# Gated linear attention, mixture of experts and SwiGLU on one core: raw weight buffers in three pools, the token-number scatters moved, idle products in the attention's tail

## The chip, the cores and the metric

The kernel runs on one core of a Trainium2 chip. The metric is the time of one execution in microseconds (us) on the device. Its engines are TensorE (PE), VectorE (DVE), ScalarE (ACT), GpSimd (POOL) and SyncE (SP), which here does nothing but issue transfers; each runs its own list of instructions in the order in which the program wrote it, and they wait for one another by semaphores. Beside them sixteen DMA engines move data between DRAM and the on-chip memory.

## The reference

Three stages, each fed by the one before: a recurrence with a decay per channel, a layer of experts in which each token goes to one expert, and a SwiGLU.

```python
def _attn_ref(r, k, v, w, u):          # 2 batches, 8 heads, 768 steps, 48 channels
    for t in range(S):
        cur = np.einsum('bhd,bhe->bhde', u[None] * kt, vt)
        y[:, :, t] = np.einsum('bhd,bhde->bhe', rt, state + cur)
        state = wt[:, :, :, None] * state + np.einsum('bhd,bhe->bhde', kt, vt)

def _moe_ref(x, w_gate, w1, w2, capacity):   # 1536 tokens x 384, 8 experts, 1024 hidden
    expert_idx = np.argmax(logits, axis=1)
    # each token takes the next row of its expert, as long as there is room
    h = np.maximum(np.einsum('ecd,edf->ecf', disp, w1), 0.0)
    y = np.einsum('ecf,efd->ecd', h, w2)
    out[i] = gate_w[i] * y[expert_idx[i], pos[i]]

def _moe2_ref(x, w_gate, w_val, w_out):      # 384 -> 1536 -> 384
    g = x @ w_gate
    silu = g * (1.0 / (1.0 + np.exp(-g)))
    return (silu * (x @ w_val) @ w_out).astype(np.float32)
```

The SwiGLU's three weight matrices arrive as 8-byte floats, all else as 4-byte ones. The result is to be as exact as float32, so each large product is made from values split in two: a high part that the fast product form takes whole, and a low part, the rest. Three products (high by high, low by high, high by low) stand for one.

## The kernel before

**The attention** works through twelve chunks of 128 tokens, six of each batch, numbered u from 0 to 11. For a chunk it loads the decay data (tiles `dm`, in turn three buffers, L291 to L295) and the values (`v`, L301), forms running products of decays on DVE (`prep1`, L325, and `prep2`, L368 to L381, which ends with the tile `rk`) and checks them, makes scores (`scores`, L415, cut to the triangle by POOL in L418), reads the state (`values`, L438 and L442), brings it forward (`state`, L454), and adds the token's own term (`own`: POOL multiplies the values by a column per head into `aV`, L395; `xrow`, L479, adds `aV` to the chunk's product on DVE, which gives the row block x). `gate_t` (L495 to L507) transposes x on PE and copies it with ACT to `xT`; in the same tile of PE's memory it can make, from `rk` and from an earlier chunk's `xT`, rows of two other results: the logits of that chunk and the columns that `own` needs (L495). `diag` (L388) makes those columns alone, 2 wide. `columns` (L526) turns the rows round. `logits` (L521) makes a chunk's logits the plain way, 8 wide. `warm` (L404) issues products whose result nobody reads.

**The choice of expert.** Chunks are grouped: 0 to 3, 4 to 7, then the pairs 8 and 9 (`two`) and 10 and 11 (`last`). For a group, DVE takes the largest logit and the weights of the choice (`choose`, from L561), PE counts the tokens of each expert by triangular products (L588, L590), and each chunk's rows, times their weight, are scattered by POOL to their places in a table in DRAM, `scr` (`scatter`, L670, an indirect DMA by the tile `slots`). Chunks 4 to 7 (`four`) are placed and scattered in the tail, behind `place(four)`; the two pairs at the very end. Expert 0 does not wait for that end: its first 240 rows are put together on chip from the rows of `scr` read back into `zrow` (`x0_load`, L721), and from the last four chunks by products with one-hot tiles (`x0_add`, L761); `parts` (L766, L767) splits the sum into the tile `xe0`.

**The branch.** Behind that each engine reads the counts and jumps to a general path if an expert has more than 240 tokens or a check has failed (L1123); with these inputs the branch is not taken.

**The experts.** For each of eight experts: `x_load` (L1155) reads its 240 rows from `scr`, `x_trans` (L1165 to L1169) transposes them in two parts on PE and splits them on ACT and DVE into `xe`; `m1` (L1180) makes eight hidden tiles, nine products each; `relu` (L1186 on ACT, L1187 on DVE) splits them into h; `m2` (L1198) takes h tile by tile, nine products each, into three results; `put_y` (L965) places these in `yT`, the stage's output with tokens in the order of the experts. So the loop runs m1(0), m2(0), m1(1), m2(1) and so on.

**The token numbers.** As `yT` is in the order of the experts, the result has to be put back in the order of the tokens. `places` (L709 to L713, four small operations on DVE) works out each token's place; `put_ids` (L1213) scatters, for one chunk of 128 tokens, their numbers (4 bytes each) to these places of a list in DRAM, `idl`: twelve scatters by POOL, three behind each of the experts 0 to 3. Behind the experts one load (`idc`, L1267) brings the list back, and the last step of the SwiGLU scatters its rows by it (L1329).

**The SwiGLU.** 36 items (p, b, f), three passes p over three blocks b of 512 tokens, four hidden tiles f in each: `gv` (L1294, 18 products), then `swiglu` and `halves` (L1300 to L1307, ACT and DVE), and the output product `outm` (L1317, 12 products) three items behind (`LAG = 3`). `part` splits a block of `yT` into tiles `yb`, from the pool `bpool`.

**The weights.** They come in 41 units: for each expert two of w1 and two of w2 (units 0 to 31), then for the SwiGLU gv0, gv1, wo0, gv2, gv3, wo1, gv4, gv5, wo2. A unit of an expert is one raw tile of 768 KB, one of the SwiGLU two. Raw tiles come in from DRAM on SP's queue (`load_raws`, L131 to L139) into the pool `rpool`, five buffers; `xe0` takes one of them as well. A raw is split in pieces into one of seven slots: ACT writes the high part (`high`, L175), DVE the low one (`low`, L180). These pieces are steps of a list, and the code places them by hand: `fill(us)` between two groups of products issues as many steps as a budget of DVE time allows, `need(key)` issues what is left of a unit before its first use, and `free(key)` gives its slot back. So all order is that of the code. Which raw is asked for where is set by two calls: in the attention's loop, `load_raws(u - 2 if u < 6 else 0)`, and in `low`, behind the last piece of a raw:

```python
        if last:
            del raw_t[r]
            load_raws(r + 5)
```

Of the kernel before, what the change touches and what calls it, by code (L numbers as in the profile page):

```python
# [24 lines left out]
HC = C // 2  # L25
# [15 lines left out]
def build(tc, cap, dm, tk, vt, ub, cst, wg, w1, w2, wgate, wval, wout, out):  # L41
# [11 lines left out]
    rpool = es.enter_context(tc.tile_pool(name="rpool", bufs=5))  # L53
# [21 lines left out]
    cnti = const.tile([128, 2 * E + 1], I32, name="cnti")  # L75

# [51 lines left out]

    def load_raws(upto):
# [47 lines left out]
    def low(i):  # L177
# [62 lines left out]

    at = ExitStack()
# [120 lines left out]
    def prep2(u):  # L362
# [3 lines left out]
        Rt = ap2.tile([128, 2, NP, HC], F32, tag="R", name="R")  # L366
# [339 lines left out]
    def places(sp):  # L706

        d1 = sp.tile([128, NU, E], F32, tag="d1", name="d1", bufs=1)
        nc.vector.tensor_tensor(out=d1, in0=pcs, in1=cf[:, E:2 * E].unsqueeze(1).to_broadcast([128, NU, E]), op=ALU.add)  # L709
        nc.vector.tensor_tensor(out=d1, in0=d1, in1=ohs, op=ALU.mult)  # L710
        d2 = sp.tile([128, NU], F32, tag="d2", name="d2", bufs=1)
# [105 lines left out]
    for u in range(NU - 2):  # L817
# [38 lines left out]
        if u >= 2:  # L856
            load_raws(u - 2 if u < 6 else 0)
# [5 lines left out]
    u = NU - 2  # L863
    four, two, last = (ended[q] for q in (7, 9, 11))
# [9 lines left out]
    expand(u)  # L874
    rows = steps.pop()
# [3 lines left out]
    gate_t(u - 1, (u + 1,))  # L879
    own(u + 1)  # L880
# [64 lines left out]
    xe0 = rpool.tile([128, 2, 3, SLOTS], F32R, tag="raw", name="xe0")  # L945
    x0_add(xhl[two[1]][1], hot[0][:, 1, :], 0)
# [54 lines left out]
    def recurrence(ydr):  # L1001
        with ExitStack() as ss:
# [12 lines left out]
            W, K, Q = (p1.tile([128, 2, S], F32, name=n) for n in ("gw", "gk", "gr"))  # L1015
# [47 lines left out]
    def general():  # L1063
        ydr = dram.tile([B, NP, 2, D, S], F32, name="ydr")
        recurrence(ydr)
        with ExitStack() as ss:
# [5 lines left out]
            xs = p0.tile([128, NU, DM], F32, name="xs")  # L1072
# [15 lines left out]
            for u in range(NU):  # L1088
# [16 lines left out]
                for f in weigh([u], sm.unsqueeze(1), [x], [xs[:, u, :]]):  # L1105
                    f()
# [323 lines left out]
```

## Time and profile before

| | |
|---|---|
| runs, median (lowest to highest) | 492.15 us (491.25 to 492.77), 3 runs |
| the profiled execution | 491.23 us, of which 489.5 us is its span, first to last instruction |
| mean granted clock of PE in it | 0.968 |
| busy in the span: PE, DVE, ACT, POOL | 96%, 68%, 49%, 15% |
| attention and choice, 0 to 111.66 us | PE busy 99.88 of the first 104.00 us |
| experts 0 and 1, 111.66 to 157.57 us | PE busy 37.78 of 45.91 us |
| experts from 157.57 to 259.21 us | PE busy 100.53 of 101.64 us |
| all transfers | 62.53 MB, mean 128 GB/s |

The page shows one execution, each time in us from its first instruction. PE counts as busy from the start of a product to its modelled end, so a busy PE isn't one at its peak: many narrow products count as much as wide ones. The granted clock is the share of full speed that PE was given. Rows of the timeline read: start, length, engine, line, operation, output <- inputs, shapes, count, and in brackets the idle time of the engine ahead of it and what ended it. Rows of the DMA issues read: output <- input, queue, kind, count, (KB each,) and us from issue to landing. Rows of the chain read: start, length, and whose work or wait it was. A row by windows gives the stretch and its length, then busy time and number of instructions of PE, its weight loads, DVE, ACT and POOL, the granted clock, the busy share of the DMA engines and their GB/s.

### The profile page before, as it was taken

The numbers are of one execution on the slowest core, as the hardware profiler recorded it, in microseconds if no ns is written. First come the engines' busy times: TensorE is split into PE (matmuls) and PEld (weight loads), VectorE is DVE, ScalarE is ACT, GpSimd is POOL, SyncE is SP. The second block draws the span as 40 slices with busy tenths as digits, with TensorE's granted clock in tenths as the row PEclk, the third lists the DMA queues.
The fourth block names the chain that finished last, engine by engine and source line by source line (L and its number), as shares of the span: only waits on it lengthen the run. The fifth ranks groups of instructions, "written<-read, shape, count | busy, mean of one in ns | idle before, by whom it ended". The sixth has DMA issues, their size and how long they took to land.

```text
span 489.5 us, 8739 instructions
## 1 busy us (share of the span) xinstructions
PE 468.8 (96%) x3271; PEld 425.2 (87%) x3274; DVE 334.4 (68%) x722; ACT 239.8 (49%) x565; POOL 73.8 (15%) x89
## 2 busy tenths in 40 slices
PE   7999999998759999999999999999999999999994
PEld 3798889988659899999998888888888888888884
DVE  8989899567448865865968986657577676533231
ACT  4465676546346957675446455353543434221110
POOL 3243437615610000000000000000000000003033
PEclk9799999769979999999999999999999999999998
DMA  7879941155989886756624232222210000001011
GB/s 234 236 233 303 309 104 68 47 178 166 167 153 298 308 274 210 227 178 214 218 66 129 86 110 66 64 66 64 66 65 1 0 1 1 0 1 64 1 65 65
DMA packets 33647, 62.53 MB, mean 128 GB/s; under 512 B 5216, under 2 KB 16992, under 8 KB 33600
## 3 DMA queue, kind: packets, MB, share of 16 engines
q1 hardware_dynamic: 31680, 57.20, 40.0%
q0 software_dynamic: 1920, 4.73, 2.7%
q8 instruction: 26, 0.43, 0.4%
q14 instruction: 21, 0.17, 0.1%
HBM read 52.48 MB, written 9.44 MB: 126 GB/s over the span
## 4 chain that ended last, share of the span: by engine, by line
PE 60%; issue 7%; DMA 3%; DVE 2%; POOL 2%; ACT 1%; another core or an unknown queue 1%; POOLq 0%; ACTq 0%; DVEq 0%
PE psg L1294 26%; PE psu L1317 12%; PE psh L1180 11%; PE pso L1198 11%; DMA raw<-in_moe_w 3%; DVE wu L180 2%; POOL out L1329 2%; PE psx L1165 1%; ACT wu L175 1%; DVE h L1187 0%; POOLq L1426 0%; ACT h L1186 0%; ACT xe L1168 0%; ACT yT L965 0%
## 5 line engine op out<-in xcount | busy, mean ns | idle before, releaser
L1294 PE MATMUL psg<-yb,wu 128*128 128x512 f32 x648 | 153.6, 391 | 0.0
L1294 PEld LDWEIGHTS psg<-yb,wu 128*128 128x128 f32 x648 | 121.2, 188 | 23.9
L1317 PE MATMUL psu<-wu,a 128*128 128x384 f32 x432 | 81.2, 337 | 0.0
L1180 PE MATMUL psh<-xe,wu 128*128 128x240 f32 x576 | 71.8, 282 | 7.6 <-DVE h L1187 6.3
L1317 PEld LDWEIGHTS psu<-wu,a 128*128 128x128 f32 x432 | 76.7, 188 | 2.7
L1180 PEld LDWEIGHTS psh<-xe,wu 128*128 128x128 f32 x576 | 68.3, 194 | 8.4 <-DVE h L1187 6.7
L1198 PE MATMUL pso<-h,wu 128*128 128x240 f32 x576 | 67.4, 275 | 1.0 <-issue 0.9
L1198 PEld LDWEIGHTS pso<-h,wu 128*128 128x128 f32 x576 | 65.6, 189 | 1.7 <-issue 1.6
L175 ACT CAST wu<-raw 128x512 fp32r<-128x512 f32 x96 | 55.7, 621 | 16.2 <-DMA raw<-in_moe_w 10.2
L180 DVE TENSOR_TENSOR wu<-raw,wu 128x512 fp32r<-128x512 f32 x96 | 61.7, 681 | 1.7 <-DVEq L1123 1.0
L1329 POOL DMA_INDIRECT out<-acc,idc x12 | 11.7, 978 | 334.3 <-DVE acc L1327 332.2
L1301 DVE TENSOR_TENSOR t<-t,psg 128x512 f32<-128x512 f32 x36 | 24.7, 685 | 51.5 <-PE psg L1294 33.7
L1306 ACT CAST a<-t 128x512 fp32r<-128x512 f32 x36 | 22.3, 619 | 56.2 <-DVE t L1301 51.8
L1187 DVE SCALAR_TENSOR_TENSOR h<-psh,h 128x240 fp32r<-128x240 f32 x64 | 24.8, 401 | 31.9 <-ACT h L1186 31.6
L175 ACT CAST wu<-bits 128x384 fp32r<-128x384 f32 x36 | 18.0, 513 | 39.9 <-DVE bits L168 39.9
L1300 ACT ACTIVATE t<-psg 128x512 f32<-128x512 f32 x36 | 21.5, 596 | 26.9 <-PE psg L1294 26.9
L1307 DVE TENSOR_TENSOR a<-t,a 128x512 fp32r<-128x512 f32 x36 | 24.7, 687 | 11.7 <-ACT a L1306 11.0
L442 PE MATMUL y<-v,A 128*128 128x48 f32 x192 | 28.8, 281 | 0.0
L1186 ACT ACTIVATE h<-psh 128x240 fp32r<-128x240 f32 x64 | 23.4, 376 | 9.7 <-PE psh L1180 9.6
L1327 DVE TENSOR_TENSOR acc<-psu,acc 128x384 f32<-128x384 f32 x24 | 12.9, 558 | 20.5 <-PE psu L1317 20.5
L442 PEld LDWEIGHTS y<-v,A 128*128 128x128 f32 x192 | 26.9, 206 | 0.0
L418 POOL TENSOR_SCALAR_AFFINE_SELECT A<-A 128x512 f32<-128x512 f32 x24 | 19.4, 831 | 22.6 <-ACT A L417 22.6
(146 smaller groups left out, 575.0 us busy)
## 6 DMA issues: line engine op xcount, KB each, us to landing
raw<-in_moe_w SPq DMA_DIRECT2D x32, 768.0 KB, 7.3
dm<-in_dm SPq DMA_DIRECT2D x18, 291.0 KB, 5.2
scr<-zrow SPq DMA_DIRECT2D x12, 384.0 KB, 7.8
raw<-in_moe_w_gate SPq DMA_DIRECT2D x6, 768.0 KB, 4.5
raw<-in_moe_w_val SPq DMA_DIRECT2D x6, 768.0 KB, 4.6
raw<-in_moe_w_out SPq DMA_DIRECT2D x6, 768.0 KB, 4.4
v<-in_tk SPq DMA_DIRECT2D x12, 192.0 KB, 6.0
dm<-in_dm SPq DMA_DIRECT2D x3, 512.0 KB, 3.7
```

The lines of the kernel that those rows point to most:

```text
L175: nc.scalar.copy(out=slot_t[u % NSLOT][:, 0, c:c + n], in_=bits[i])
L180: nc.vector.tensor_tensor(out=w[:, 1, c:c + n], in0=bits.pop(i), in1=R(w[:, 0, c:c + n]), op=ALU.subtract)
L442: nc.tensor.matmul(y[:, c0:c0 + D], A[:, g, p, :], V[:, c0:c0 + D], start=not u % UPB, stop=True, skip_group_check=True)
L1180: nc.tensor.matmul(ps, w[:, a, k, c0:c0 + 128], xet[e][:, b, k, :], start=n == 0, stop=n == 8)
L1186: nc.scalar.activation(out=h[:, 0, :], in_=ps, func=AF.Relu)
L1187: nc.vector.scalar_tensor_tensor(out=h[:, 1, :], in0=ps, scalar=0.0, in1=R(h[:, 0, :]), op0=ALU.max, op1=ALU.subtract)
L1198: nc.tensor.matmul(ypt[e, d], w[:, a, f % 4, 128 * d:128 * d + 128], h[:, b, :], start=f == 0 and n == 0, stop=f == 7 and n == 2)
L1294: nc.tensor.matmul(gps[i][g], w[:, a, g, k, c0:c0 + 128], yb[t, k][:, c], start=a_ == k == 0, stop=a_ == k == 2)
L1301: nc.vector.tensor_tensor(out=t, in0=t, in1=pg[1], op=ALU.mult)
L1306: nc.scalar.copy(out=a[:, 0], in_=t)
L1307: nc.vector.tensor_tensor(out=a[:, 1], in0=t, in1=R(a[:, 0]), op=ALU.subtract)
L1317: nc.tensor.matmul(out_ps[t, j], att[i][:, c, 128 * j:128 * j + 128], w[:, a, f % 4, :], start=f % FP == 0 and n == 0, stop=f % FP == FP - ...
```

## The change

**Buffers for raws.** `RAWS = 5, 2, 3`. The pool of five stays (four for raws from the start, the fifth is `xe0`, and joins them once m1 of expert 0 is done); a second pool of two stands from the attention's start; a third of three opens in the attention's tail, at u = 10, in the memory of the decay tiles (`dm`, their anchors, `wm`, R), which have moved to a pool of their own that ends there. `load_raws` now loads whenever any pool has a buffer whose raw is fully split. The calls in the attention's loop ask for raws 0 to 5 at chunks 4 to 7; behind the opening of the third pool one call asks for all it can hold. From expert 4 on the second and third pools take no more raws, and when their last is split they end and `bpool` takes memory there. `hpool`, for h, goes from 11 to 9 buffers.

**Token numbers.** `places` moves from m1 of expert 0 to SwiGLU item 4, the twelve scatters to items 5 to 10, two each, and the load of `idc` to item 13. The tiles that `places` needs become constants, and the table of Silu, which ACT loaded by an operation on `cf`, is loaded by one on a small tile `lut`. `x_load(1)` moves from inside m1 of expert 0 to ahead of it.

**The attention's tail.** Two idle products ahead of `values(10)` and two ahead of `values(11)`; `gate_t(9, rows=(8, 11))` makes rows (for the logits of chunk 8 and the columns of chunk 11) in place of `diag`, so that `columns` follows later, `own(11)` behind it, and `logits(8)` is dropped.

**The general path** uses memory of `yT` in place of tiles of its own.

```diff
+RAWS = 5, 2, 3
...
+    rps, done = [[rpool, RAWS[0] - 1, []]], set()
+
+    def more_raws(n):
+        life = ExitStack()
+        rps.append([life.enter_context(tc.tile_pool(name=f"raws{len(rps)}", bufs=n, side="right")), n, []])
+        lives.append(life)
...
     def load_raws(upto):
         while st["loaded"] < min(upto, len(raws_)):
+            free_ = [p for p in rps if len(p[2]) < p[1] or p[2][-p[1]] in done]
+            if not free_:
+                return
+            free_[0][2].append(st["loaded"])
             src = raws_[st["loaded"]]
-            t = raw_t[st["loaded"]] = rpool.tile([128, 1536], F32, tag="raw", name="raw")
+            t = raw_t[st["loaded"]] = free_[0][0].tile([128, 1536], F32, tag="raw", name="raw")
...
         if last:
             del raw_t[r]
-            load_raws(r + 5)
+            done.add(r)
+            ended_raws()
+            load_raws(len(raws_))
...
+    more_raws(RAWS[1])
     at = ExitStack()
...
+    early = ExitStack()
+    ep = early.enter_context(tc.tile_pool(name="ep", bufs=2, side="right"))
+    dmt = [ep.tile([128, DMW], F32, name=f"dm{i}", bufs=1) for i in range(3)]
...
-        if u >= 2:
-            load_raws(u - 2 if u < 6 else 0)
+        if u >= 4:
+            load_raws(2 * (u - 4) + 1)
...
     u = NU - 2
+    early.close()
+    more_raws(RAWS[2])
+    load_raws(len(raws_))
...
     expand(u)
+    warm(2, ps1)
     rows = steps.pop()
     flush()
     rows()
     values(u, range(2))
-    gate_t(u - 1, (u + 1,))
-    own(u + 1)
+    gate_t(u - 1, rows=(u - 2, u + 1))
     count(four)
...
     values(u, range(2, NP))
+    columns(u - 1, u - 2, u + 1)
+    own(u + 1)
     xrow(u)
-    logits(u - 2)
     judge()
     fill(2.4, 3.0)
+    warm(2, ps1)
     values(u + 1)
...
     xe0 = rpool.tile([128, 2, 3, SLOTS], F32R, tag="raw", name="xe0")
+    rps[0][1] += 1
+    rps[0][2].append("xe0")
...
-    hpool = mo.enter_context(tc.tile_pool(name="hpool", bufs=11))
+    hpool = mo.enter_context(tc.tile_pool(name="hpool", bufs=9))
...
     xet[0] = xe0
+    x_load(1)
     for e in range(E):
+        if e == 4:
+            end_raws()
...
-            if not e and f == 3:
-                places(xp)
             fill(0.5)
-            if not e and f == 4:
-                x_load(1)
         if not e:
+            done.add("xe0")
             reg = off_reg(e)
...
-        for j in range(3 * e, min(3 * e + 3, NU)):
-            put_ids(j)
...
-    nc.sync.dma_start(out=idc, in_=idl.rearrange("(j p) o -> p (j o)", p=128), allow_slow_non_contiguous=True)
...
+        if i == 4:
+            places()
+        if 4 < i < 11:
+            put_ids(2 * i - 10)
+            put_ids(2 * i - 9)
+        if i == 13:
+            nc.sync.dma_start(out=idc, in_=idl.rearrange("(j p) o -> p (j o)", p=128), allow_slow_non_contiguous=True)
         fill(1.2)
```

What the change makes of the engines' lists is shown at three places. The first is SP's list at the end of the attention, from the third raw on, toward the branch; `raw` is a tile of raw weights, `dm` the decay data, `v` the values, and `zrow` the rows of `scr` for expert 0. Before:

```order
L137 DMA raw<-in_moe_w 128x4x384
L295 DMA dm_101<-in_dm 48x1552 x2
L301 DMA v<-in_tk 128x384
L295 DMA dm_102<-in_dm 48x1552 x2
L301 DMA v<-in_tk 128x384 x2
L721 DMA zrow<-scr 128x384
L721 DMA zrow<-scr 112x384
L137 DMA raw<-in_moe_w 128x4x384
L137 DMA raw<-in_moe_w 128x3x512
```

With the change:

```order
L168 DMA raw<-in_moe_w 128x4x384
L331 DMA dm_110<-in_dm 48x1552 x2
L337 DMA v<-in_tk 128x384
L168 DMA raw<-in_moe_w 128x4x384
L168 DMA raw<-in_moe_w 128x3x512
L331 DMA dm_111<-in_dm 48x1552 x2
L337 DMA v<-in_tk 128x384
L168 DMA raw<-in_moe_w 128x3x512
L337 DMA v<-in_tk 128x384
L168 DMA raw<-in_moe_w 128x4x384 x2
L168 DMA raw<-in_moe_w 128x3x512
L755 DMA zrow<-scr 128x384
```

The first row of each is raw 2. Before, raws 3 and 4 stood behind the reads of `scr`; now raws 3 to 8 stand ahead of them, the last three behind the chunks' last loads, and raw 9 behind the second read.

The second place is POOL's list from the attention's last triangle to the last scatters of rows. Before:

```order
L418 AFFINE_SELECT A<-A 128x512 x2
L395 TENSOR_TENSOR aV<-v,xT 128x384
L670 DMA scr<-xg,slots 3072x384 x4
L753 TENSOR_TENSOR xhl<-xg,xhl 128x384
L670 DMA scr<-xg,slots 3072x384 x4
```

With the change:

```order
L454 AFFINE_SELECT A<-A 128x512 x2
L706 DMA scr<-xg,slots 3072x384 x4
L431 TENSOR_TENSOR aV<-v,a_1418 128x384
L787 TENSOR_TENSOR xhl<-xg,xhl 128x384
L706 DMA scr<-xg,slots 3072x384 x4
```

The product `aV` of the last chunk has gone behind the four scatters, and takes its column from a tile of its own (`a_1418`) in place of `xT`.

The third is PE's list in the tail, from the last scores (`psA`) to the first count of the four chunks (L588, now L624). Before:

```order
L415 MATMUL psA<-M 128x128 x8
L438 MATMUL y<-Sb_107,M 128x96
L442 MATMUL y<-v,A 128x48 x2
L438 MATMUL y<-Sb_107,M 128x96
L442 MATMUL y<-v,A 128x48 x2
L388 MATMUL psx<-ud,rk 128x2 x4
L501 MATMUL psx<-ident,x 128x128 x3
L588 LDWEIGHTS tri
```

With the change:

```order
L451 MATMUL psA<-M 128x128 x8
L440 LDWEIGHTS ones
L440 MATMUL psW<-xinit,ones 128x512
L440 LDWEIGHTS ones
L440 MATMUL psW<-xinit,ones 128x512
L474 MATMUL y<-Sb_116,M 128x96
L478 MATMUL y<-v,A 128x48 x2
L474 MATMUL y<-Sb_116,M 128x96
L478 MATMUL y<-v,A 128x48 x2
L531 MATMUL psx<-xT,wgs 16x128 x3
L531 MATMUL psx<-rk,ud 16x128 x4
L537 MATMUL psx<-ident,x 128x128 x3
```

Two idle products came in ahead of the first half of chunk 10's reads of the state, and seven products 128 wide (of float32, each of which PE runs as two) stand where four that are 2 wide stood.

More of the change, by code (lines that the diff above doesn't have):

```diff
@@ L52, in build @@
     wpool = es.enter_context(tc.tile_pool(name="wpool", bufs=1))
-    rpool = es.enter_context(tc.tile_pool(name="rpool", bufs=5))
+    rpool = es.enter_context(tc.tile_pool(name="rpool", bufs=RAWS[0]))
     es.enter_context(tc.manual_schedule())
@@ L75, in build @@
     cnti = const.tile([128, 2 * E + 1], I32, name="cnti")
+    d1 = const.tile([128, NU, E], F32, name="d1")
+    d2 = const.tile([128, NU], F32, name="d2")
+    lut = const.tile([128, 1], F32, name="lut")
     def v1(e, j):
@@ L127, in wu, with end_raws, ended_raws @@
         return slot_t[unit_of[key] % NSLOT]
+    rps, done = [[rpool, RAWS[0] - 1, []]], set()
[3 more added lines that the diff above has]
+        lives.append(life)
+    lives, ending = [], []
+    def end_raws():
+        ending.extend(rps[1:])
+        del rps[1:]
+    def ended_raws():
+        if ending and all(r in done for p in ending for r in p[2]):
+            ending.clear()
+            while lives:
+                lives.pop().close()
+            after_raws()
     def load_raws(upto):
         while st["loaded"] < min(upto, len(raws_)):
+            free_ = [p for p in rps if len(p[2]) < p[1] or p[2][-p[1]] in done]
+            if not free_:
+                return
+            free_[0][2].append(st["loaded"])
             src = raws_[st["loaded"]]
-            t = raw_t[st["loaded"]] = rpool.tile([128, 1536], F32, tag="raw", name="raw")
+            t = raw_t[st["loaded"]] = free_[0][0].tile([128, 1536], F32, tag="raw", name="raw")
             if len(src.shape) == 3 and src.dtype != F32:
@@ L256, in build @@
     odds = ac.tile([128, 1], BF16, name="odds")
-    dmt = [ac.tile([128, DMW], F32, name=f"dm{i}") for i in range(3)]
-    anch = [ac.tile([128, 2 * (NP * HC + G - 1)], F32, name=f"anch{i}") for i in range(2)]
-    wm = [ac.tile([128, 2, NP, HC], F32, name=f"wm{i}") for i in range(2)]
+    early = ExitStack()
+    ep = early.enter_context(tc.tile_pool(name="ep", bufs=2, side="right"))
+    dmt = [ep.tile([128, DMW], F32, name=f"dm{i}", bufs=1) for i in range(3)]
+    anch = [ep.tile([128, 2 * (NP * HC + G - 1)], F32, name=f"anch{i}", bufs=1) for i in range(2)]
+    wm = [ep.tile([128, 2, NP, HC], F32, name=f"wm{i}", bufs=1) for i in range(2)]
     Sb = [ac.tile([128, NP, 2 * D], F32, name=f"Sb{i}") for i in range(2)]
@@ L365, in prep2 @@
             return
-        Rt = ap2.tile([128, 2, NP, HC], F32, tag="R", name="R")
+        Rt = ep.tile([128, 2, NP, HC], F32, tag="R", name="R")
         for h in range(2):
@@ L1014, in recurrence @@
                                   allow_slow_non_contiguous=True)
-            W, K, Q = (p1.tile([128, 2, S], F32, name=n) for n in ("gw", "gk", "gr"))
+            W, K, Q = (yT[i][:, 0:2 * S].rearrange("p (a t) -> p a t", a=2) for i in range(3))
             T = p1.tile([128, 2, S + 1], F32, name="gs")
@@ L1071, in general @@
             pp = ss.enter_context(tc.tile_pool(name="gq", bufs=1, space=PSUM))
-            xs = p0.tile([128, NU, DM], F32, name="xs")
+            xs = [yT[u // 4][:, DM * (u % 4):DM * (u % 4) + DM] for u in range(NU)]
             wgs = p0.tile([128, 3, E], F32, name="wgs")
@@ L1139, in build, with after_raws @@
     NB, TB = 3, 512
-    bpool = es.enter_context(tc.tile_pool(name="bpool", bufs=2))
+    bpools = []
+    def after_raws():
+        bpools.append(es.enter_context(tc.tile_pool(name="bpool", bufs=2, side="right")))
     mo = ExitStack()
     xp = mo.enter_context(tc.tile_pool(name="xp", bufs=2))
-    hpool = mo.enter_context(tc.tile_pool(name="hpool", bufs=11))
+    hpool = mo.enter_context(tc.tile_pool(name="hpool", bufs=9))
     psX = mo.enter_context(tc.tile_pool(name="psX", bufs=1, space=PSUM))
@@ L1206, in part @@
             return
-        y = yb[t, k] = bpool.tile([128, 2, TB], F32R, tag=f"yb{k}", name="yb")
+        y = yb[t, k] = bpools[0].tile([128, 2, TB], F32R, tag=f"yb{k}", name="yb")
         src = yT[k][:, TB * (t % NB):TB * (t % NB) + TB]
@@ L1253, in build @@
                 if (e, f) == (3, 4):
-                    nc.scalar.activation(out=cf, in_=cf, func=AF.Silu)
+                    nc.scalar.activation(out=lut, in_=ident[:, 0:1], func=AF.Silu)
                 fill(0.9 if e else 0.7)
```

8 lines of the change are left out of this document (3 added, 5 removed).

## The prediction

> **What bounds the kernel now.** I read the page first: the span, then its 40 slices.
>
> ```profile
> span 489.5 us, 8739 instructions
> PE   7999999998759999999999999999999999999994
> ...
> DMA  7879941155989886756624232222210000001011
> ```
>
> TensorE (PE) is busy in almost every slice, so time can be won only where PE waits or runs slowly. A slice is 12.2 us. Slices 10 to 12 (from 0: about 122 to 159 us) are the one place late in the program where PE falls to 7 and 5; the DMA is full there, but nearly empty in slices 6 and 7 (73 to 98 us), in the attention. So I cut the trace by windows at the borders of PE's groups: m1 and m2 of experts 0, 1 and 2, then a settled expert, then SwiGLU.
>
> ```profile
> 111.66:120.43 8.77, 8.56 (x73) 8.33 (x73) 6.24 (x16) 5.90 (x14) 3.87 (x5) 1.00 0.42 145
> 120.43:133.23 12.80, 10.06 (x80) 8.98 (x79) 5.77 (x12) 4.64 (x11) 9.18 (x9) 1.00 0.94 189
> 133.23:149.50 16.27, 11.09 (x80) 10.90 (x79) 8.91 (x18) 7.37 (x19) 1.99 (x2) 0.79 0.94 145
> 149.50:157.57 8.07, 8.07 (x74) 8.07 (x73) 7.02 (x14) 5.51 (x11) 0.00 (x0) 1.00 1.02 343
> 157.57:167.84 10.27, 9.16 (x82) 8.96 (x81) 7.36 (x16) 9.36 (x24) 0.00 (x0) 1.00 0.92 315
> 167.84:184.64 16.80, 16.80 (x152) 16.80 (x152) 12.38 (x26) 11.19 (x27) 0.00 (x0) 1.00 0.81 277
> 259.21:443.81 184.60, 184.60 (x884) 161.80 (x883) 126.25 (x250) 81.31 (x159) 0.00 (x0) 1.00 0.15 46
> ```
>
> Columns: length, busy time of PE, weight load, DVE, ACT, POOL, then granted clock, DMA share, GB/s. From 167.84 on PE has no gap. m2(0) takes 12.80, m1(1) 16.27 and m1(2) 10.27 us. What they should take is in the chain of waits, which also says what holds them:
>
> ```profile
> 122.11 3.60 another core or an unknown queue
> 133.22 16.39 DMA raw<-in_moe_w
> 167.84 8.08 PE pso L1198 x72
> 175.92 3.02 PE psh L1180 x27
> 178.94 0.33 PE psx L1165 x3
> ```
>
> A settled m2 is 72 products in 8.08 us; a settled m1 with two groups of transposes runs from 175.92 to 184.64, 8.72 us; one group is 0.33 or, by the border of the next, 0.3 us. The 16.39 us are transfers of raw weights. Counting transfers from 0 (raw n is weight unit n), raw 7 is issued at 122.40 and its first cast, which waits for it, runs at 140.26:
>
> ```profile
> 122.40 0.38 SPq L137 DMA_DIRECT2D raw<-in_moe_w  x1
> 140.26 0.62 ACT L175 CAST wu<-raw 128x512 fp32r<-128x512 f32 x1 [6.16 <-DMA raw<-in_moe_w]
> raw<-in_moe_w_out SPq DMA_DIRECT2D x6, 768.0 KB, 4.4
> idl<-ids,dests POOLq DMA_INDIRECT x12, 12.4
> scr<-xg,slots POOLq DMA_INDIRECT x12, 2.7
> 118.36 1.18 POOL L1213 DMA_INDIRECT idl<-ids,dests  x1 [3.99 <-DVE dests L713]
> 138.32 0.97 POOL L1213 DMA_INDIRECT idl<-ids,dests  x1 [3.11 <-DMA idl<-ids,dests]
> ```
>
> Some 17.5 us (the cast's wait ends then, so the transfer does), against 4.4 for the same size later. Meanwhile the DMA is busy at 0.94 and moves 145 to 189 GB/s; from 149.50 at 1.02 it moves 343. What ends there are the twelve token-number scatters, issued 118.36 to 138.32 and 12.4 us under way (so to about 150.7) for 128 words of 4 bytes each; a scatter of whole rows lands in 2.7. So two things make the weights late: they are asked for late (raw 5 only after the branch, while slices 6 and 7 are idle), and they share the DMA with scatters that occupy it and move nothing.
>
> The Trainium skill (DMA: Bandwidth & Descriptors, Specifications) says that transfers under 512 B are done as read-modify-write. The trace agrees as far as it goes: 12.4 us against 2.7.
>
> **The change part by part.** *Raw weights.* By the order, raws 0 to 8 stand ahead of the last scr read and raw 9 right behind it; before, only raws 0 to 2 did. Raws 6 to 8 take the decay tiles' memory and so wait for the last product rk and the last check there:
>
> ```profile
> 85.66 0.68 DVE L381 TENSOR_TENSOR rk<-dm 128x512 f32<-128x512 f32 x1
> 99.79 0.80 SPq L721 DMA_DIRECT2D zrow<-scr  x2
> 108.02 1.49 PE L761 MATMUL x<-ident,zrow 128*128 128x128 f32 x12
> ```
>
> They issue at about 86.4 and move 3 x 0.786 MB; at the 343 GB/s above, 6.9 us, so they have landed by some 95, ahead of the read of scr at 99.79 that x0 needs at 108.02. Raw 9 follows at about 101. At m1(0) everything for experts 0 and 1 and half of 2 is on chip. Raw 10 (m2 of expert 2) then has from about 117 until about 146; even 17.5 us would do. What SP's queue holds up behind raw 6's new wait is only raws 7 and 8 and that read, none due before 99.8.
>
> *Token numbers moved.* Four small DVE operations, twelve scatters and one load leave experts 0 to 3 for SwiGLU items 4 to 13. POOL is idle there (0.00 busy in the last window above), and the DMA moves 46 GB/s. DVE has 126.25 busy of 184.60 us.
>
> ```profile
> 117.04 0.26 DVE L709 TENSOR_TENSOR d<-pcs,cf 128x96 f32<-128x96 f32 x1
> 286.96 0.37 SPq L135 DMA_DIRECT2D raw<-in_moe_w_out  x1
> ```
>
> The four operations are no longer than their first, 0.26, so about 1 us. An item is 30 products; the window's 884 are 29.5 items, 6.3 us each, and the output product runs three items behind, so the 1 us has some 18 us of cover; without it, it would cost 1 us. If weights took 17.5 us there as well, they would still be early: the last raw for the second pass's output product is asked for at 286.96, and that product comes with item 15, near 350. I take nothing.
>
> *The sum over the first experts.* With weights present, m2(0) is 8.08 + 2 x 0.31 = 8.70 instead of 12.80: 4.10 won. m1(1): 8.72 for 16.27, 7.55 won. m2(1): 8.07, nothing. m1(2): 8.72 for 10.27, 1.55 won. Together **13.2 us**. Next late would be the splitting of weights on DVE:
>
> ```profile
> 151.85 6.10 DVE L180 TENSOR_TENSOR wu<-raw,wu 128x512 fp32r<-128x512 f32 x10
> ```
>
> 0.61 us a piece. The longest run without a relu between is 13 pieces in m2(1) (by the order), 7.9 us within 8.07; in the trace the same run began late because its raws did, which is m1(2)'s lost 1.55. m1(0) keeps its 8.77: it uses raws that were there before. hpool with 9 buffers instead of 11 holds one expert's eight and one; each is read by m2 before m1 of the next expert writes it, so nothing.
>
> *The attention's tail.* Here the change gives and takes.
>
> ```profile
> 89.42:92.83 3.41, 3.41 (x44) 3.40 (x43) 1.81 (x10) 3.41 (x9) 0.94 (x2) 1.00 0.00 0
> 92.83:96.24 3.41, 3.41 (x18) 3.41 (x18) 1.79 (x3) 0.78 (x2) 2.72 (x3) 0.50 0.19 71
> 103.07:106.48 3.41, 3.41 (x21) 1.94 (x19) 3.34 (x22) 1.32 (x4) 1.04 (x1) 0.50 0.98 328
> 81.42 1.04 PE L495 MATMUL psx<-rk,ud 128*16 128x128 f32 x8
> 88.86 1.02 PE L388 MATMUL psx<-ud,rk 128*128 128x2 f32 x8
> 91.93 0.83 POOL L395 TENSOR_TENSOR aV<-v,xT 128x384 f32<-128x384 f32 x1 [2.40 <-ACT xT L507]
> 92.91 1.42 POOL L670 DMA_INDIRECT scr<-xg,slots  x1 [0.15 <-issue]
> 97.19 0.98 POOL L670 DMA_INDIRECT scr<-xg,slots  x1 [0.30 <-issue]
> 97.60 0.56 DVE L479 TENSOR_TENSOR x<-y,aV 128x384 f32<-128x384 f32 x1 [2.98 <-PE y L442]
> 101.71 1.29 PE L521 MATMUL lg<-wgs,xT 128*128 128x8 f32 x6
> 102.98 1.87 PE L404 MATMUL psW<-xinit,ones 128*128 128x512 bf16 x4
> 103.03 0.17 DVE L561 TENSOR_REDUCE mx<-lg 128x2 f32<-128x16 f32 x1 [1.83 <-PE lg L521]
> ```
>
> The clock is halved from 92.83 to 106.48, exactly four windows of 3.41 us, after a window in which PE counted as busy but held many products 2 or 8 columns wide (the eight of L388, the counts). Two idle products per place (four took 1.87 us at half clock, so 0.23 each at full clock) and 14 gate products of 0.11 us (eight of L495 less their common latency) instead of eight narrow ones fill that window: they cost 0.46 + 14 x 0.11 - 0.9 (L388) = 1.1 us before the counts and should hold the clock until values(11) is done. But POOL now issues its four scatters (5.26 us from 92.91 to 98.17) ahead of aV of chunk 11: x(11), which ran at 97.60 when PE's y was there, now waits for aV, 0.83 behind 98.2, so to about 99.2. Behind it stand its own 0.56, its transposes, a logits group, idle products, its own logits and the last choice (before: 103.03). At half clock that is 99.75 + 0.9 (transposes) + 1.29 + 0.9 + 1.29 = 104.1, some 1.0 lost; at full clock the four last terms halve but for latencies, 0.45 + 0.75 + 0.46 + 0.75, which gives 102.2, 0.8 won. PE is nearly empty from 97 to 99.8, so a fall about 99.7 is likely: I take 0.2 us lost, ends 1.0 won and 2.7 lost (1.0, and half of one more window of 3.41 us at half clock).
>
> The Trainium skill (TensorE: Matmul & The Clock Gate, Part 1) has a free-running window of 3413 ns, half clock after an idle window and full clock after a busy one. The spacing agrees to the hundredth; but here the clock fell after a window with 3.41 of 3.41 us busy, so what counts is not the profile's busy time. By that rule two products of 0.23 us make no busy window and cannot bring a fallen clock back: the sum would take the half-clock end, 1.0 lost.
>
> **Sum.** 13.2 - 0.2 = 13.0 us off a span of 489.5: 476.5. The profiled execution took 491.23, 1.7 around its span: 478.2. The median of the runs, 492.15, lies 0.9 above that execution: **479.1 us**.
>
> **Rivals.**
> 1. *The waits at expert 0's xe are not the DMA's.* ACT waited 3.60 us on a queue that the trace does not name. It happened while the scatters ran, and no later expert shows it; but if it is the first write of a new tile after the branch, the 4.10 of m2(0) stay: 483.2. 13%.
> 2. *The clock falls in the tail and returns a window late.* 2.7 us lost there: 481.6. For it: PE's empty stretch before x(11); against: the row 103.07:106.48 shows that the warm products and the first x0 products suffice to bring it back. 9%.
> 3. *The weights still come late*, since the cause is neither the late asking nor the scatters (a DMA slow beside reads of scr, say): only the tail moves, 492.3. Against: 343 GB/s from 149.50 with the same kinds of loads. 4%.
> 4. *Slower: the scr scatters suffer beside raws 6 to 8 as the token-number scatters did beside raws.* Place: x0, which needs zrow. Four scatters end on POOL at 98.2; with 12.4 us to land and 17.5 for the read behind them zrow is there at 128, 20 us after 108.0: less 13.2, some 7 slower, 499. It decides once scatter and read together take over 9.8 us (from 98.2 to 108.0), and turns the sign at 23. Against: rows of 1536 bytes land in 2.7, and raws 6 to 8 should be in by 95. 3%.
>
> **How the numbers follow.** The forecast, from 477 to 480.5, has 68%; the rivals above 29%; 3% go to a better tail below 477. Range **476.5 to 483.5**: it reaches over rivals 1 and 2, the bounds of the tail and of m2(0), and leaves out rivals 3 and 4 and the better tail, 1 in 10. About 0.3% (1.5 us) is what a measurement here can tell from no change: faster 0.94, within it 0.03, slower 0.03.
>
> **What would show it.** Right: no cast of a raw waits for DMA before 160 us; m2(0), m1(1) and m1(2) near 8.7 each; about 300 GB/s, not 3, between 87 and 95 us; the token-number scatters at 270 to 320 us with PE gapless; x(11) about 1.6 us later on DVE, waiting for aV. Wrong: zrow's products after 108.5, a gap of PE in SwiGLU, or attention chunks 9 to 11 starting later because their dm sits behind two raws.

## The result, and the profile after

| | before | after |
|---|---|---|
| median of the runs | 492.46 us (491.25 to 495.65, 4 runs) | 479.25 us (478.62 to 481.66, 4 runs) |
| ratio after to before | | 0.9731, 95% interval 0.9673 to 0.9789 |
| profiled execution, its span | 491.23, 489.5 us | 481.66, 479.9 us |
| mean granted clock in it | 0.968 | 0.980 |

The change makes the kernel 2.7% faster; 479.1 us was predicted. The profiled execution of after happens to be the slowest of its four runs, so it shows 9.6 us of the 13.2 that lie between the medians. The head of its page, span, PE and DMA by 40 slices (12.0 us each):

```profile
span 479.9 us, 8741 instructions
...
PE   7999999979999999999999999999999999999994
...
DMA  7798995642989974325524244133100000001011
```

PE's weak slices 10 and 11 (7 and 5 before) are gone; the weak one that is left is slice 8 (96 to 108 us), in the attention's tail, and the DMA works in slices 6 and 7 already. By windows at the borders of the groups (same columns as in the prediction), m1(0), m2(0), m1(1), m2(1), m1(2) and the SwiGLU of after:

```profile
113.59:121.79 8.20, 8.20 (x73) 8.20 (x73) 6.50 (x14) 6.21 (x14) 2.06 (x2) 1.00 0.50 149
121.79:130.50 8.71, 8.71 (x81) 8.71 (x79) 7.20 (x13) 6.44 (x15) 0.00 (x0) 1.00 0.95 295
130.50:139.20 8.70, 8.70 (x81) 8.70 (x79) 6.75 (x16) 6.95 (x18) 0.00 (x0) 1.00 0.84 271
139.20:147.28 8.08, 8.08 (x75) 8.08 (x74) 8.08 (x16) 7.20 (x16) 0.00 (x0) 1.00 0.88 293
147.28:155.99 8.71, 8.71 (x80) 8.71 (x79) 6.43 (x15) 6.64 (x17) 0.00 (x0) 1.00 1.05 381
247.29:479.90 232.61, 226.61 (x1082) 197.15 (x1080) 141.80 (x278) 88.23 (x171) 25.14 (x24) 1.00 0.17 47
```

and the SwiGLU of before:

```profile
259.05:489.50 230.45, 224.24 (x1082) 197.41 (x1080) 140.90 (x274) 88.18 (x171) 11.74 (x12) 0.99 0.15 48
```

m2(0), m1(1) and m1(2) take 8.71, 8.70 and 8.71 us; the prediction had 8.70, 8.72 and 8.72. DVE is busy for all 8.08 us of m2(1), as the prediction said it would be, and PE does not wait for it. But the SwiGLU takes 232.61 us where it took 230.45, and that was not predicted. The page shows where, in its groups of instructions (busy time, mean ns of one, idle time ahead); before and after:

```profile
L1294 PE MATMUL psg<-yb,wu 128*128 128x512 f32 x648 | 153.6, 391 | 0.0
L1317 PE MATMUL psu<-wu,a 128*128 128x384 f32 x432 | 81.2, 337 | 0.0
```

```profile
L1336 PE MATMUL psg<-yb,wu 128*128 128x512 f32 x648 | 156.3, 395 | 0.0
L1359 PE MATMUL psu<-wu,a 128*128 128x384 f32 x432 | 80.8, 336 | 0.0
```

The same 648 products of gv, without a gap between them, take 4 ns more each, 2.7 us of busy time in all; those of the output product give 0.4 back. What the scatters of token numbers do in after is in POOL's timeline (the first and the last of twelve) and in the DMA issues:

```profile
273.39 1.10 POOL L1258 DMA_INDIRECT idl<-ids,dests  x1 [157.44 <-DVE bits L186]
288.95 1.24 POOL L1258 DMA_INDIRECT idl<-ids,dests  x1 [0.30 <-issue]
```

```profile
idl<-ids,dests POOLq DMA_INDIRECT x12, 7.7
raw<-in_moe_w_out SPq DMA_DIRECT2D x6, 768.0 KB, 4.3
```

They go in one burst, land in 7.7 us in place of 12.4, and the raws of `w_out` land as they did (4.3 us, before 4.4). The tail, from the timelines of POOL and DVE (last of the four row scatters, aV and x of chunk 11, the last choice):

```profile
97.64 0.98 POOL L706 DMA_INDIRECT scr<-xg,slots  x1 [0.30 <-ACT xT L543]
98.63 0.86 POOL L431 TENSOR_TENSOR aV<-v,a 128x384 f32<-128x384 f32 x1
99.52 0.56 DVE L515 TENSOR_TENSOR x<-y,aV 128x384 f32<-128x384 f32 x1 [3.70 <-POOL aV L431]
104.10 0.17 DVE L597 TENSOR_REDUCE mx<-lg 128x2 f32<-128x16 f32 x1 [1.83 <-PE lg L557]
```

x(11) runs at 99.52 and waits 3.70 us for aV (99.2 was worked out), and the last choice starts at 104.10 (104.1 for the half-clock end). Two windows of after show the early raws and the clock there:

```profile
89.00:93.00 4.00, 4.00 (x47) 3.58 (x45) 1.21 (x8) 3.05 (x7) 0.50 (x1) 1.00 1.06 389
91.00:113.00 22.00, 18.86 (x145) 16.42 (x145) 12.69 (x63) 9.43 (x24) 7.74 (x8) 0.77 0.46 159
```

389 GB/s move from 89 to 93 us, where nothing moved before; over the tail the granted clock is 0.77, so 10 of 22 us ran at half. Cut into windows of 1 us, the half clock lasts from about 99.2 to 109.5; before, it lasted from 92.83 to 106.48. The balance of the two profiled executions, in us: start of m1(0) +1.93, m1(0) -0.57, m2(0) -4.09, m1(1) -7.57, m1(2) -1.40, SwiGLU +2.16, the rest of the experts -0.06: together -9.6.

### The profile page after: what moved, and what is told of

Same layout as the page of the kernel before. It is cut to its first block, busy times and chain, and to the rows that moved or that the text cites. A ratio compares the mean times of both kernels' runs of the same rounds, so it can differ in the third digit from the quotient of the medians.

```text
span 479.9 us, 8741 instructions
## 1 busy us (share of the span) xinstructions
PE 466.4 (97%) x3280; PEld 420.5 (88%) x3280; DVE 334.9 (70%) x722; ACT 241.0 (50%) x567; POOL 73.6 (15%) x89
## 4 chain that ended last, share of the span: by engine, by line
PE 72%; issue 2%; POOL 1%; DVE 0%; POOLq 0%
PE psg L1336 31%; PE psu L1359 14%; PE psh L1225 14%; PE pso L1243 13%; POOL out L1371 1%; PE psx L1210 1%; DVE acc L1369 0%; POOLq L1475 0%; POOLq L1371 0%
## 5 line engine op out<-in xcount | busy, mean ns | idle before, releaser
L1336 PE MATMUL psg<-yb,wu 128*128 128x512 f32 x648 | 156.3, 395 | 0.0
L1225 PE MATMUL psh<-xe,wu 128*128 128x240 f32 x576 | 68.9, 277 | 1.1 <-ACTq L1164 1.1
L1225 PEld LDWEIGHTS psh<-xe,wu 128*128 128x128 f32 x576 | 66.1, 190 | 1.3 <-ACTq L1164 1.3
L1243 PE MATMUL pso<-h,wu 128*128 128x240 f32 x576 | 66.4, 275 | 0.0
L1258 POOL DMA_INDIRECT idl<-ids,dests x12 | 13.4, 1120 | 160.8 <-DVE bits L186 157.4
L478 PE MATMUL y<-v,A 128*128 128x48 f32 x192 | 27.6, 273 | 0.0
L478 PEld LDWEIGHTS y<-v,A 128*128 128x128 f32 x192 | 25.7, 198 | 0.0
```

Source lines behind the costliest of these rows:

```text
L478: nc.tensor.matmul(y[:, c0:c0 + D], A[:, g, p, :], V[:, c0:c0 + D], start=not u % UPB, stop=True, skip_group_check=True)
L1225: nc.tensor.matmul(ps, w[:, a, k, c0:c0 + 128], xet[e][:, b, k, :], start=n == 0, stop=n == 8)
L1243: nc.tensor.matmul(ypt[e, d], w[:, a, f % 4, 128 * d:128 * d + 128], h[:, b, :], start=f == 0 and n == 0, stop=f == 7 and n == 2)
L1336: nc.tensor.matmul(gps[i][g], w[:, a, g, k, c0:c0 + 128], yb[t, k][:, c], start=a_ == k == 0, stop=a_ == k == 2)
```

## The experiments

Three questions were open. Which of the two causes made the weights late, the late asking or the scatters? What makes the SwiGLU slower? And what is the tail worth? All kernels ran beside runs of before on the same chip; each ratio is to those.

**Only the token numbers moved** (moved_ids). Before, with this change and its counterpart in the SwiGLU, and no other:

```diff
-            if not e and f == 3:
-                places(xp)
...
-        for j in range(3 * e, min(3 * e + 3, NU)):
-            put_ids(j)
...
+        if i == 4:
+            places()
+        if 4 < i < 11:
+            put_ids(2 * i - 10)
+            put_ids(2 * i - 9)
```

> The kernel before with nothing but the token numbers moved: places, the twelve scatters and the load of idc in SwiGLU items 4 to 13; raws are asked for where they were, the tail is as before. Theory (two causes, the scatters are the stronger one): raw 5 to 9, still issued from about 117 us on, land in some 4.4 us each, so that m2(0) takes about 8.7, m1(1) 8.7 to 10, m1(2) 8.7 us: 479.5 to 483 us. Rival (the late asking is the cause): the waits of m1(1) and m1(2) stay nearly whole, 488 to 492 us.

Measured: 479.38 us (476.57 to 479.61), ratio 0.9735 (0.9675 to 0.9795): as much as the whole change wins. m2(0), m1(1), m1(2) and the SwiGLU by windows:

```profile
118.91:127.61 8.70, 8.70 (x80) 8.70 (x79) 7.21 (x13) 6.42 (x15) 0.00 (x0) 1.00 1.03 362
127.61:136.33 8.72, 8.72 (x81) 8.72 (x80) 6.75 (x16) 7.01 (x18) 0.00 (x0) 1.00 0.91 321
144.40:153.12 8.72, 8.72 (x80) 8.72 (x79) 6.44 (x15) 6.62 (x17) 0.00 (x0) 1.00 0.93 311
244.51:474.90 230.39, 224.29 (x1082) 197.40 (x1080) 141.74 (x278) 88.17 (x171) 25.16 (x24) 1.00 0.18 48
```

and from ACT's timeline the only two casts of raws that waited for the DMA in these stages:

```profile
126.70 0.62 ACT L177 CAST wu<-raw 128x512 fp32r<-128x512 f32 x1 [0.42 <-DMA raw<-in_moe_w]
142.82 1.14 ACT L177 CAST wu<-raw 128x512 fp32r<-128x512 f32 x2 [0.73 <-DMA raw<-in_moe_w]
```

Raws asked for as late as before come in time once the DMA moves 362 GB/s instead of 189. Raw 7, asked for at 120.08, is there at 126.70, 6.6 us later; before it took 17.9 (122.40 to 140.26). The late asking alone costs nothing in these stages, and the SwiGLU, with the scatters in it, takes 230.39 us for 230.45.

Why raw 7 mattered is worth a look, as m1(1) does not use it: it is the second half of w2 of expert 1. In ACT's list its first cast (140.26, in the prediction) stands ahead of m1(1)'s relus, so PE waited for those:

```profile
142.94 4.20 PE L1180 MATMUL psh<-xe,wu 128*128 128x240 f32 x18 [5.18 <-DVE h L1187]
```

**Only the raws early** (early_raws). After, with places, scatters and idc where they were in before:

```diff
+            if not e and f == 3:
+                places()
...
+        for j in range(3 * e, min(3 * e + 3, NU)):
+            put_ids(j)
...
-        if i == 4:
-            places()
-        if 4 < i < 11:
-            put_ids(2 * i - 10)
-            put_ids(2 * i - 9)
```

> The changed kernel with the token numbers put back: places in m1(0), three scatters behind each of experts 0 to 3, idc behind the experts. Theory (each of the two causes alone makes the weights late only in part): raws 0 to 9 are on chip ahead of the scatters, so m1(1) and m2(1) keep 8.7 and 8.1 us; what still comes beside the scatters is xr of expert 1 and raw 10 on, so m2(0) keeps up to 4.1 us of its wait and m1(2) up to 1.6: 480 to 485 us. Rival (the scatters alone are the cause, and everything beside them waits): over 488 us. Rival (the late asking alone is): 479 us, no wait at all.

Measured: 489.05 us (486.02 to 494.09), ratio 0.9928 (0.989 to 0.9966): some 3 us won of the 13, where 480 to 485 us was expected. m2(0) and m1(1) by windows:

```profile
119.02:133.98 14.96, 11.56 (x80) 11.37 (x79) 6.58 (x13) 5.37 (x12) 9.73 (x10) 0.77 0.88 166
133.98:142.68 8.70, 8.70 (x80) 8.70 (x79) 7.34 (x16) 7.49 (x21) 1.54 (x2) 1.00 0.86 170
```

a relu and the two parts of xe in ACT's timeline, and the products of gv:

```profile
121.28 0.37 ACT L1231 ACTIVATE h<-psh 128x240 fp32r<-128x240 f32 x1 [2.19 <-remote]
125.77 0.48 ACT L1213 CAST xe<-psx 128x384 fp32r<-128x384 f32 x1 [3.61 <-remote]
131.59 0.44 ACT L1213 CAST xe<-psx 128x336 fp32r<-128x336 f32 x1 [3.79 <-remote]
L1341 PE MATMUL psg<-yb,wu 128*128 128x512 f32 x648 | 156.3, 395 | 0.0
```

m1(1) is whole at 8.70, and m1(2) at 8.71, as the raws are there: for these two, asking early is enough as well. But m2(0) takes 14.96, longer than the 12.80 of before, with ACT's waits on something the trace does not name. So the scatters, left in place, cost PE some of their time elsewhere. Part of what is missing is not theirs: m1(3) takes 9.93 us for 8.72, waiting for its rows of `scr`, and the products of gv take 395 ns here too, with no scatter in the SwiGLU, which takes 232.7 us.

**Half of the scatters put back** (half_ids). moved_ids, with places in m1(0) and the calls of six scatters behind experts 0 and 1:

```diff
+            if not e and f == 3:
+                places()
...
+        for j in range(3 * e, min(3 * e + 3, NU // 2)):
+            put_ids(j)
...
-        if i == 4:
-            places()
-        if 4 < i < 11:
+        if 7 < i < 11:
```

> moved_ids with half of the token-number scatters put back: places in m1(0), three scatters each behind experts 0 and 1, the other six in SwiGLU items 8 to 10. Theory (each scatter costs its share of the DMA): the slow stretch is half as long, about 118 to 134 us, so m2(0) keeps about 4 us of its wait and m1(1) loses up to 4: 483 to 487 us. Rival (the first few scatters hide, only a full queue of them holds the transfers up): 479.4 to 481 us.

Measured: 491.07 us (484.83 to 493.94), ratio 0.9979 (0.9935 to 1.0022): all of the gain gone, not half. POOL's timeline has the reason (first and last of the twelve):

```profile
117.35 1.17 POOL L1213 DMA_INDIRECT idl<-ids,dests  x1 [2.69 <-DVE dests L713]
136.89 0.97 POOL L1213 DMA_INDIRECT idl<-ids,dests  x1 [3.27 <-DMA idl<-ids,dests]
```

m2(0) and m1(1) by windows:

```profile
120.16:128.87 8.71, 8.71 (x81) 8.71 (x79) 6.79 (x13) 3.95 (x9) 6.88 (x7) 1.00 0.88 143
128.87:149.37 20.50, 10.97 (x80) 10.77 (x79) 7.28 (x15) 8.32 (x21) 3.40 (x4) 0.75 0.99 166
```

and the longest piece of the chain of waits there:

```profile
121.39 18.84 DMA raw<-in_moe_w
```

All twelve ran from 117 to 138 us, the six called in the SwiGLU too: nothing stands ahead of them in POOL's list but a wait for dests, the result of places. The run did not do what it was made for, so how the cost grows with the number of scatters stays open. It shows three other things. It is places, not put_ids, whose place in the code sets when the scatters run. With the load of idc left in the SwiGLU all of the gain is gone, so that load was not the cause; it is the scatters (places itself is four DVE operations, some 1 us). And the same scatters left m2(0) whole (8.71) and took 11.8 us from m1(1), where early_raws lost 6.3 in m2(0) and nothing in m1(1). Where the time is lost differs; that it is lost is common.

**yb at multiples of 64 bytes** (yb_aligned). After, with 32 bytes kept free at the right end:

```diff
+    edge = es.enter_context(tc.tile_pool(name="edge", bufs=1, side="right"))
+    edge.tile([128, 8], F32, name="pad")
```

> The changed kernel with 32 bytes per partition kept free at the right end of the on-chip memory, so that yb starts at a multiple of 64 bytes again, as before the change (the change put it 32 bytes off). In the profile of the change an item of the SwiGLU takes 6.29 us where it took 6.225. Theory (the place of yb against multiples of 64 bytes sets it): 18 products of gv go from 4.36 back to 4.28 us, 36 items win 2.2 us: about 477 us. Rival (something else, as the memory's other end or the other tiles' places): 4.36 stays, 479 us.

Measured: 481.95 us (478.95 to 482.73), ratio 0.9774 (0.9725 to 0.9824). A miss: 477 was expected, and the products stay long, so it is not the 64 bytes.

```profile
L1338 PE MATMUL psg<-yb,wu 128*128 128x512 f32 x648 | 156.6, 395 | 0.0
```

**yb at the right end, nothing else** (moved_yb_right). moved_ids with this:

```diff
-    bpool = es.enter_context(tc.tile_pool(name="bpool", bufs=2))
+    bpool = es.enter_context(tc.tile_pool(name="bpool", bufs=2, side="right"))
```

> The kernel with only the token numbers moved (moved_ids, 479.38 us), and yb's pool at the right end of the memory, at the very addresses that it has in the changed kernel. Theory (yb's place there makes the products of gv longer, whatever the raws do): their mean goes from 391 to 395 ns, 18 of them from 4.28 to 4.36 us, and the time by 2.2 to 2.7 us: 481.5 to 482.5 us. Rival (the raws' pools, the split of hpool or their end at expert 4 on make them longer): 391 ns and 479.4 us.

Measured: 480.96 us (478.21 to 482.2), ratio 0.9768 (0.9709 to 0.9827). The time's interval does not tell it from moved_ids, but the products do:

```profile
L1289 PE MATMUL psg<-yb,wu 128*128 128x512 f32 x648 | 156.4, 395 | 0.0
```

Without any new pool of raws they take 395 ns once yb lies where the change puts it, against 391 in moved_ids, and the SwiGLU takes 232.8 us against 230.39.

**A third of yb at the right end** (moved_yb_split), and **the other tiles in another order** (swapped_tiles). Both are moved_ids with one edit:

```diff
+    bright = es.enter_context(tc.tile_pool(name="bright", bufs=2, side="right"))
...
-        y = yb[t, k] = bpool.tile([128, 2, TB], F32R, tag=f"yb{k}", name="yb")
+        y = yb[t, k] = (bpool if k else bright).tile([128, 2, TB], F32R, tag=f"yb{k}", name="yb")
```

```diff
-    apool = sw.enter_context(tc.tile_pool(name="apool", bufs=4))
     tpool = sw.enter_context(tc.tile_pool(name="tpool", bufs=2))
+    apool = sw.enter_context(tc.tile_pool(name="apool", bufs=4))
```

> moved_ids with the two yb tiles of k=0 alone at the right end of the memory and those of k=1 and 2 on the left. Theory (a product is longer where the operand that it moves lies at the right end): only the 6 of 18 products with k=0 grow, by some 7 ns each, a third of the 2.2 us: mean 392 ns, 480.2 us. Rival (it hangs on what else lies where, as the tiles that ACT and DVE write meanwhile): all 18 grow or none.

> moved_ids with the pools of the SwiGLU in the other order: t and acc below, the split tiles a on top; yb stays where it was. Theory (how long a product of gv takes hangs on where the tiles lie that ACT, DVE and PE use beside it, not on yb's own place): their mean leaves 391 ns by 2 or more, and psu's 337 too. Rival (yb's place alone): 391 and 337 ns stay, 479.4 us.

Measured: 480.83 us (480.09 to 481.58) and 476.45 us (475.26 to 477.63), two runs each. The groups of moved_yb_split, then of swapped_tiles:

```profile
L1290 PE MATMUL psg<-yb,wu 128*128 128x512 f32 x648 | 155.5, 394 | 0.0
```

```profile
L1289 PE MATMUL psg<-yb,wu 128*128 128x512 f32 x648 | 153.6, 391 | 0.0
L1312 PE MATMUL psu<-wu,a 128*128 128x384 f32 x432 | 81.2, 337 | 0.0
```

Exchanging a and t changes nothing here; moving some of yb does, and to 394 ns, not the 392 that a third of the products would give. In moved_yb_split the starts of an item's products, averaged over the items, are 230 to 234 ns apart for k = 0, 1 and 2 alike (in moved_ids 226 to 232), so it is not simply the tile that a product reads. The length hangs on where the yb tiles lie; by what rule stays open.

**The tail** (moved_tail, moved_tail_own, own_first). moved_tail is moved_ids with the changed tail:

```diff
+    warm(2, ps1)
...
-    gate_t(u - 1, (u + 1,))
-    own(u + 1)
+    gate_t(u - 1, rows=(u - 2, u + 1))
...
+    columns(u - 1, u - 2, u + 1)
+    own(u + 1)
     xrow(u)
-    logits(u - 2)
...
+    warm(2, ps1)
```

own_first is after, and moved_tail_own is moved_tail, with aV ahead of the scatters:

```diff
     tick(4)
+    columns(u - 1, u - 2, u + 1)
+    own(u + 1)
     for q in (*ready, *four):
...
-    columns(u - 1, u - 2, u + 1)
-    own(u + 1)
     xrow(u)
```

> The changed kernel with columns and own(11) moved ahead of the four scatters of rows on POOL, so that aV of chunk 11 doesn't wait for them. Theory (the 3.70 us that x(11) waits for aV set the start of the experts): x(11) runs at about 96.8 instead of 99.5, m1(0) starts 2 to 4 us earlier: 475 to 477.5 us. Rival (the halved clock or the choice behind it sets that start anyway): 478.5 to 480 us. Rival (the scatters, 0.3 to 0.8 us later, delay zrow): 479.5 us or more, and the products with zrow wait for it.

> moved_ids and the changed tail (four idle products, rows in place of diag, aV of chunk 11 behind the scatters), without the two new pools of raws. Theory (the raws' pools win nothing and cost 2.7 us in the SwiGLU by yb's place; what moves the changed kernel level with moved_ids is the tail and m1(0)): 476 to 478 us. Rival (the tail is worth nothing, as predicted 0.2 lost): 479 to 480 us.

> moved_tail with columns and own(11) ahead of the four scatters. Theory (x(11)'s 3.7 us wait for aV goes and the clock falls for one window of 3.41 us rather than three): 1 to 3 us less than moved_tail, 474.5 to 476.5 us. Rival (where the clock falls in an execution decides, not aV): the same as moved_tail within 0.7 us.

Measured: own_first 479.65 us (477.37 to 485.69), ratio 0.9738 (0.9684 to 0.9793); moved_tail 479.57 us (476.68 to 480.2), 0.9733 (0.9687 to 0.9779); moved_tail_own 477.48 us (476.52 to 480.68), 0.9727 (0.9682 to 0.9771). So the changed tail wins nothing over moved_ids (479.38), where 476 to 478 was expected; own_first wins nothing that can be measured over after; moved_tail_own looked better, by 2.1 us, but not beyond its interval. In its profile the wait for aV is gone, and part of the lead is lost again behind it. The timelines of DVE, POOL and PE (x(11), a step of the choice, POOL beside it, the first product of m1(0)):

```profile
96.01 0.56 DVE L481 TENSOR_TENSOR x<-y,aV 128x384 f32<-128x384 f32 x1 [0.51 <-PE y L444]
100.84 1.01 DVE L535 TENSOR_SCALAR sm<-sm 128x2 f32<-128x2 f32 x1
100.78 1.05 POOL L753 TENSOR_TENSOR xhl<-xg,xhl 128x384 fp32r<-128x384 f32 x1 [3.06 <-ACT xg L748]
109.11 3.09 PE L1182 MATMUL psh<-xe,wu 128*128 128x240 f32 x18 [2.66 <-DVEq L1125]
```

and the windows of the tail and of m1(0):

```profile
91.00:113.00 22.00, 18.14 (x151) 16.47 (x152) 14.79 (x66) 10.50 (x26) 9.88 (x10) 0.94 0.47 163
109.11:118.87 9.76, 9.76 (x72) 9.76 (x73) 6.26 (x14) 5.57 (x13) 1.16 (x2) 0.83 0.45 163
```

x(11) runs at 96.01 where after has 99.52, and the clock over the tail is 0.94 for 0.77. But PE then waits 2.66 us at the branch (1.15 in after; the trace names no more than DVE's sequencer there), and m1(0) runs at a clock of 0.83 and takes 9.76 us for 8.20: the fall of the clock has moved into it. The step of the choice that takes 1.01 us, and 0.17 at 98.56, ends as POOL's operation does; before has such a one beside POOL as well (1.08 us at 104.49), so it is not what this tail lost.

**Both once more on one chip** (after_again and tail_own_again are the changed kernel and moved_tail_own).

> The changed kernel once more, beside tail_own_again on the same chip: 479 to 480 us, with single runs from 478 to 482 as the clock falls early or late in the tail.

> moved_tail_own once more, beside after_again on the same chip. Theory (2.2 to 2.7 us of the SwiGLU come back without the raws' pools, and x(11) doesn't wait for aV): 1 to 2.5 us under after_again. Rival (the first measurement was the luck of the clock): within 0.7 us of it.

Measured: after_again 479.43 us (478.37 to 482.48), ratio 0.9786 (0.9748 to 0.9824); tail_own_again 477.94 us (475.6 to 480.11), 0.9744 (0.9707 to 0.9781). The second is 1.5 us under the first by the medians, as 1.8 (479.25 less 477.48) by the first measurements of both; the intervals of the ratios overlap, so this order, found twice, is likely and not certain. It is the fastest version that was measured twice, without any new pool, and beats before by 2.6%.

What the tail does is best read at the end of m1(0), since an early start is partly lost in m1(0) itself: it takes 8.19 to 9.78 us, with waits of up to 0.54 us for split weights in some profiles, and with a granted clock of 0.83 in the four that take 9.76 us or more. This end scatters by up to 4.5 us between kernels with the same tail, as the clock falls early or late. In moved_yb_right the granted clock is at half from about 93.8 to 107.4, in swapped_tiles, which differs from it only behind the branch, it is full until about 108.1.

| tail | end of m1(0) in the profiles, us | mean |
|---|---|---|
| as before (6 kernels) | 120.43, 118.91, 121.18, 120.95, 120.16, 117.63 | 119.9 |
| as changed (5) | 121.79, 119.02, 123.01, 121.80, 118.49 | 120.8 |
| changed, aV first (3) | 117.50, 118.87, 117.92 | 118.1 |

## Why the prediction was right, point by point

**The sum over the first experts, 13.2 us, held**: 4.09, 7.57 and 1.40 us were won where 4.10, 7.55 and 1.55 stood (the prediction ended m1(2) at 167.84, 0.16 behind the first product of m2(2)). This is nearly all of the change's worth.

**"Two things make the weights late" was half right.** In m1(1) and m1(2) it takes both: they are whole without the scatters (moved_ids) and whole with early raws beside the scatters (early_raws). But the prediction named the late asking first and took the new pools for a part of the gain. moved_ids has neither new pool nor earlier asking, and wins the same; early_raws has both and wins 3 us, as m2(0) is not helped by them and yb's place costs its 2.2. So moving the scatters is sufficient here, and asking early is not. The evidence was in the prediction's own rows: 17.5 us for a raw that takes 4.4, at a DMA share of 0.94 with 189 GB/s. (The low slices of the prediction's row are 10 and 11, not 10 to 12; nothing hangs on it.)

**"I take nothing" for the SwiGLU was right for the scatters and wrong for the whole.** Moved there, the scatters cost PE nothing (moved_ids: 391 ns, 230.39 us). But what the change says of memory, that bpool goes where the raws were, was never priced: yb's new place lengthens 648 products by 4 ns and the SwiGLU by 2.16 us in the profiles. This is the term that was missing, and it is the price of pools that win nothing that could be measured once the scatters are gone.

**m1(0) was taken to keep 8.77** and took 8.20 us; 8.19 in after_again, but 8.84 in own_first and 9.08 in yb_aligned, which have the same pools. Its 0.57 us comes and goes with the tail ahead of it.

**The tail, 0.2 lost with ends +1.0 and -2.7**: by the ends of m1(0) it loses 0.9 in the mean of the profiles, which their scatter does not tell from nothing. In single executions the start of m1(0) moved both ways: 1.93 lost in the profile of after, 1.36 won in that of after_again (110.30). That x(11) would wait for aV, that the clock would fall in PE's gap around it, and the time of the last choice at half clock came as worked out. By the Trainium skill (TensorE: Matmul & The Clock Gate, Part 1) the window runs freely, so that the same program meets it at another phase each time. The 117.6 to 121.2 of one and the same tail agree with that.

So the first experts won 13.1 us, and the SwiGLU gave 2.2 back: 10.9, or 11.5 with m1(0). What is left to the 13.2 between the medians lies within the tail's scatter, and before's own median was 490.92 to 492.12 us in the later runs; beside the 490.92, after_again wins 11.5. That the median came within 0.2 us of the forecast is luck: a miss of 2.2 us that this scatter hid. The mechanism of the 13.2, PE's waits in m2(0), m1(1) and m1(2) going, is not luck; it shows in the profile stage by stage.

**The rivals.** The first (the waits for xe stay) did not come true in after, which writes the same tiles behind the branch without such a wait, and nor does moved_ids have one; so it is not the first write of a new tile. But early_raws had them back at 3.61 and 3.79 us and half_ids, with the same scatters, had none. What they wait for is not settled. The second came true in part, in the profiled execution: the clock came back at about 109.5, where before it did at 106.48, and 1.93 us were lost where the rival had 2.7; in after_again it came back at about 105.2. The third fell with moved_ids. The fourth fell too: zrow landed 2.5 us after its issue, and the scatters of rows in 3.0. Its products started at 109.94 rather than 108.02, behind the 108.5 that the prediction gave as a sign of being wrong, but with PE busy right up to them, so what came late was the tail ahead of them, at half clock. The other signs went the prediction's way: no cast of a raw waits for the DMA before 160 us, and rk of the last chunk runs at 85.63 us (before 85.66), so no chunk was late for its dm. The scatters of token numbers ran at 273 to 290 us, not spread over items 5 to 10, for the reason that half_ids shows.

## What to carry to other kernels

A full DMA share at half the usual GB/s was not a shortage of bandwidth here: look for transfers of few bytes among the large ones, and move them before making room to ask earlier. Where nothing else stands ahead of an operation in its engine's list, it is moved by what it waits for, not by the line that issues it. And a step that waits for data of later use, as the cast of raw 7, holds up the steps behind it in the list that are needed now. When buffers are moved to make room, compare the mean duration of each group of products before and after, even those without a gap.

## What the runs showed that was not expected

Twelve scatters of 128 words of 4 bytes, in all 6 KB, cost 12.5 us beside loads of weights (491.88 to 479.38) and nothing in the SwiGLU, where the DMA moves 48 GB/s. The duration of the 512-wide products depends, reproducibly to the nanosecond over kernels, on where the yb tiles lie on the chip (391, 394 or 395 ns); a shift of 32 bytes did not matter to it, and exchanging the tiles written meanwhile didn't either. One list of instructions met the tail's end 3.5 us apart in two kernels that differ only behind it (121.18 in moved_yb_right, 117.63 in swapped_tiles).
